# Half of a weight block moved behind a run of shuffle transfers on the load queue

## The chip, the core and the metric

The kernel runs on one core of a Trainium2 chip. Its engines work side by side: TensorE (PE; PEld is its weight load), VectorE (DVE), ScalarE (ACT), GpSimd (POOL) and SyncE (SP). Each has its own instruction list, and semaphores order them against each other. Transfers are issued by SyncE or by GpSimd and carried out by 16 DMA engines. The metric is the device time of one execution in microseconds; of several executions the median is given.

## The reference

The input x has 2048 positions of 448 channels, and so have k and v, all bf16. First comes a mixer: x + A(layernorm(x), k, v), with

```
k_shift[t] = sum over 4 taps of k[t - tap] * shift_k[tap]
kv         = k_shift * v
y          = causal convolution of kv with ssm_k along the 2048 positions, by a 4096-point FFT
A          = q * (y + kv * ssm_D)
h          = x + A(layernorm(x), k, v)
```

Then comes an MLP over positions rather than over channels:

```
u  = gelu(w1^T layernorm(h) + b1)     w1: 2048 x 1792
h2 = h + w2^T u + b2                  w2: 1792 x 2048
```

w1 and w2 are 7.34 MB each, in bf16. They are the bulk of what is read from memory.

## The kernel before, in words

The 2048 positions are laid out as 128 partitions by 16 rows. Everything lies in one large on-chip array, `arena`, so nearly all tiles are called `arena` in the profile; PSUM tiles are called `ps`.

The convolution is a two-stage Fourier transform by matrix products. A first stage works within each row (L933 for k, L885 and its neighbours for v), and its result is spread anew over the partitions by small transfers from on-chip memory to on-chip memory, the shuffles (L947). A second stage follows (L964). Then the spectra are multiplied on VectorE (L1015) and the first inverse stage runs on TensorE (L1027). ScalarE or VectorE copies its result out of PSUM (L652), and a second set of shuffles carries it to the buffer TZ. These are the inverse shuffles (L1037): 16 blocks, each with one transfer of 196 KB on GpSimd's queue and one of 28 KB on SyncE's. Every block writes a few partitions of all rows of TZ, so the second inverse stage (L1104) can begin on row 0 only when all blocks have arrived. To keep TensorE running meanwhile, 34 matmuls without a consumer (L1047) stand ahead of L1104.

After each row of the inverse transform, ScalarE and VectorE apply the gate and the residual (L1111, L1118), and with GpSimd's help the second layernorm (ending at L1159, which writes Q). The MLP's first product runs over 14 blocks of 128 output features. The first seven, from the left half of w1 (buffer W1A, 16 rows of 896 columns), are accumulated together: for each row, seven matmuls (L1203) that read that row of W1A and of Q. They are mixed with L1104 as rows of Q are completed. The other seven blocks, from the right half (W1B), follow one at a time, each over all 16 rows (L1213). Gelu is on ScalarE (L1193). The second product, 16 x 14 matmuls from W2, follows (L1223), then bias and residual (L1227) and the output transfers (L1231, L1234).

All weights are loaded by SyncE: W1A in four pieces of four rows (L1178), W1B in four (L1181), W2 in four (L1188). W1A is loaded before the inverse shuffles, W2 and W1B behind them.

The order of instructions on each engine comes from a planner that runs when the kernel is built. Each operation carries a due time, `sch.t0`. An engine takes, of the operations whose predecessors are done in the planner's model, the one with the highest priority:

```
prio[o.id] = prio[o.id] * 1e-6 - o.t0
```

so the earlier due time goes first, and the length of the path behind an operation only breaks ties. The argument `after` adds predecessors by hand. In `emit_w1_load` these come from `shuf`, which holds the shuffles by name: `shuf["upool15"]` is the last of GpSimd's shuffles of v's transform, and `shuf["zpool"]` the last of its inverse shuffles. The constants that matter here:

```
T_Q, T_DQ, T_I2, T_DI2, T_M1, T_W1 = 83.98, 14.35, 85.76, 0.401, 102.98, 122.45
T_CP, T_XL, T_WB = 20.0, -35.53, 154.44
```

W2's loads are due at T_W1 + 4.0 = 126.45 and wait for `shuf["zpool"]`. The numbers are only sort keys; they are not microseconds of the run.

Of the kernel before, what the change touches and what calls it, by code (L numbers as in the profile page):

```python
# [509 lines left out]
def _build(nc, A_q, A_k, A_v, A_shift_k, A_ssm_k, A_ssm_D, B_w1, B_b1, B_w2, B_b2, out):  # L510
# [27 lines left out]
    o_W1A = 0  # L538
# [27 lines left out]
    with ctx:  # L566
        sch = _Sched(nc, ctx, n_dma_sems=112, small_off=SMALL)
# [73 lines left out]
        T_Q, T_DQ, T_I2, T_DI2, T_M1, T_W1 = 83.98, 14.35, 85.76, 0.401, 102.98, 122.45  # L641

        T_TH, T_TN = -36.0, -30.0
        T_CP, T_XL, T_WB = 20.0, -35.53, 154.44
# [309 lines left out]
        shuf = {}  # L954
# [217 lines left out]

        def emit_w1_load(which):
            for h in range(4):
                sch.t0 = (T_W1, T_WB)[which] + 0.1 * h * (1 - which)
                rs = slice(4 * h, 4 * h + 4)
                if which == 0:
                    op(WQ, lambda e, W, rs=rs: e.dma_start(W1A[:, rs, :], w1d[:, rs, 0:896]),  # L1178
                       w=[(o_W1A + 4 * h * 1792, 4 * 1792)], dmab=128 * 4 * 1792, after=[shuf["upool15"]])
                else:  # L1180
                    op(WQ, lambda e, W, rs=rs: e.dma_start(W1B[:, rs, :], w1d[:, rs, 896:1792]),  # L1181
                       w=[(o_W1B + 4 * h * 1792, 4 * 1792)], dmab=128 * 4 * 1792, after=[shuf["zpool"]])
# [14 lines left out]
        def emit_mlp():  # L1197
# [21 lines left out]
            for r in range(R):  # L1219
# [19 lines left out]
                ("u1", emit_stage1, (V, o_V, TU, o_TU, "u")),    # L1239
                ("xload", emit_xload, ()), ("ct", emit_ct, ()), ("bias", emit_bias, ()), ("q", emit_q, ()),  # L1240
                ("u2", emit_stage2, (TU, o_TU, None)), ("i1", emit_products_i1, ()), ("w1a", emit_w1_load, (0,)), ("w1b", emit_w1_load, (1,)),
                ("warm", emit_warm, (N_WZ, T_I2 - 50.0, lambda: i1_last[-1:])),
                ("i2", emit_i2, ()), ("w2", emit_w2_load, ()), ("mlp", emit_mlp, ()))
# [39 lines left out]
```

## Time and profile before

| what | value |
|---|---|
| median of five runs | 191.09 us (189.79 to 191.66) |
| the profiled execution's own time | 191.09 us |
| its span, first to last instruction | 189.2 us |
| PE busy | 177.9 us (94%) |
| DVE busy | 110.0 us (58%) |
| ACT busy | 97.3 us (51%) |
| POOL busy | 72.1 us (38%) |
| mean granted TensorE clock | 0.973 |
| bytes moved by DMA | 35.43 MB, mean 187 GB/s |
| weight loads of W1 (L1178 and L1181) | 8 of 896 KB, median 13.1 us from issue to landing |
| weight loads of W2 (L1188) | 2 of 2048 KB, 10.4 us; 2 of 1536 KB, 17.5 us |

Times in the trace run from the first instruction. Busy time of PE is that of matmuls, which overlap, so 94% doesn't mean that 94% of its peak is reached. The page also shows the span in 40 slices of 4.73 us each, with the DMA engines' traffic in GB/s per slice. An engine's idle time before an instruction is put down to what ended it; that is the view that tells what waits for what.

### The profile page before, as it was taken

The numbers are of one execution on the slowest core, as the hardware profiler recorded it, in microseconds if no ns is written. First come the engines' busy times: TensorE is split into PE (matmuls) and PEld (weight loads), VectorE is DVE, ScalarE is ACT, GpSimd is POOL, SyncE is SP. The second block draws the span as 40 slices with busy tenths as digits, with TensorE's granted clock in tenths as the row PEclk, the third lists the DMA queues.
The fourth block names the chain that finished last, engine by engine and source line by source line (L and its number), as shares of the span: only waits on it lengthen the run. The fifth ranks groups of instructions, "written<-read, shape, count | busy, mean of one in ns | idle before, by whom it ended". The sixth has DMA issues, their size and how long they took to land.

```text
span 189.2 us, 2824 instructions
## 1 busy us (share of the span) xinstructions
PE 177.9 (94%) x1033; PEld 93.8 (50%) x1033; DVE 110.0 (58%) x181; ACT 97.3 (51%) x141; POOL 72.1 (38%) x176
## 2 busy tenths in 40 slices
PE   7999999899888998899989999999999999999993
PEld 2754443333332343234425444555556777777771
DVE  8867679898788999999788756100000222212221
ACT  3493979998799989970888384352121000000000
POOL 8933967799550015579169757000000000000000
PEclk9995599999999999999999999999999999999999
DMA  5996487778638998775799999000000100111111
GB/s 159 416 419 248 126 246 218 216 205 244 200 110 295 378 386 288 211 226 165 242 418 418 422 403 403 34 0 0 0 0 3 49 19 29 49 52 49 49 49 49
DMA packets 15724, 35.43 MB, mean 187 GB/s; under 512 B 3869, under 2 KB 9886, under 8 KB 15710
## 3 DMA queue, kind: packets, MB, share of 16 engines
q1 hardware_dynamic: 11102, 25.59, 35.9%
q0 software_dynamic: 4608, 9.66, 17.8%
q8 instruction: 8, 0.13, 0.3%
q14 instruction: 6, 0.05, 0.1%
HBM read 22.37 MB, written 1.84 MB: 128 GB/s over the span
## 4 chain that ended last, share of the span: by engine, by line
PE 82%; ACT 8%; DVE 6%; issue 2%
PE ps L1223 22%; PE ps L1213 11%; PE ps L1203 10%; PE ps L933 7%; PE ps L885 6%; PE ps L1047 5%; PE ps L1027 5%; ACT arena L652 4%; PE ps L964 3%; PE ps L1104 3%; PE ps L914 3%; PE ps L904 3%; ACT arena L943 2%; DVE arena L1015 2%; PE ps L996 1%
## 5 line engine op out<-in xcount | busy, mean ns | idle before, releaser
L1227 DVE SCALAR_TENSOR_TENSOR arena<-ps,arena 128x448 bf16<-128x448 f32 x16 | 10.9, 684 | 56.9 <-PE ps L1223 56.9
L1223 PE MATMUL ps<-arena 128*128 128x448 bf16 x224 | 42.5, 353 | 0.0
L1223 PEld LDWEIGHTS ps<-arena 128*128 128x128 bf16 x224 | 32.3, 144 | 10.1
L943 ACT CAST arena<-ps 128x896 bf16<-128x896 f32 x32 | 26.8, 930 | 5.7 <-PE ps L937 2.9
L652 ACT CAST arena<-ps 128x896 bf16<-128x896 f32 (+1 forms) x26 | 22.0, 909 | 2.9 <-PE ps L868 1.9
L1203 PE MATMUL ps<-arena 128*128 128x448 bf16 x112 | 23.0, 353 | 0.3 <-DVE arena L1159 0.2
L947 POOL DMA_DIRECT2D arena<-arena x32 | 19.2, 601 | 9.2 <-ACT arena L943 6.0
L1213 PE MATMUL ps<-arena 128*128 128x448 bf16 x112 | 21.4, 352 | 0.0
L933 PE MATMUL ps<-arena 128*128 128x448 bf16 x64 | 18.9, 416 | 0.4 <-ACT arena L943 0.2
L1193 ACT ACTIVATE arena<-ps,arena 128x448 bf16<-128x448 f32 x14 | 8.2, 639 | 20.1 <-PE ps L1213 14.7
L879 DVE TENSOR_TENSOR arena<-arena 128x1792 bf16<-128x1792 bf16 x16 | 18.3, 1178 | 0.0
L964 PE MATMUL ps<-arena 128*64 128x448 bf16 x128 | 16.4, 362 | 1.8 <-ACT arena L652 1.0
L1111 ACT ACTIVATE arena<-ps,arena 128x448 f32<-128x448 f32 x16 | 11.2, 722 | 12.0 <-PE ps L1104 9.0
L1037 POOL DMA_DIRECT2D arena<-arena x16 | 9.4, 594 | 20.8 <-PE ps L964 15.6
L1015 DVE TENSOR_TENSOR arena<-arena 128x1792 bf16<-128x1792 bf16 x16 | 16.4, 1083 | 0.0
L1203 PEld LDWEIGHTS ps<-arena 128*128 128x128 bf16 x112 | 10.9, 98 | 11.1 <-DVE arena L1159 1.3
L1213 PEld LDWEIGHTS ps<-arena 128*128 128x128 bf16 x112 | 10.9, 98 | 10.2
L885 PE MATMUL ps<-arena 128*128 128x448 bf16 x64 | 14.5, 354 | 1.5 <-ACT arena L943 0.9
L1027 PE MATMUL ps<-arena 64*128 64x448 bf16 x128 | 14.1, 352 | 1.3 <-DVE arena L1015 0.6
L1118 DVE SCALAR_TENSOR_TENSOR arena<-arena 128x448 f32<-128x448 bf16 x16 | 10.7, 677 | 4.5 <-ACT arena L1111 4.5
L933 PEld LDWEIGHTS ps<-arena 128*128 128x128 f16 x64 | 6.3, 109 | 10.0 <-issue 4.2
L964 PEld LDWEIGHTS ps<-arena 128*64 128x64 f16 x128 | 5.4, 108 | 11.4 <-ACT arena L652 4.6
(87 smaller groups left out, 206.0 us busy)
## 6 DMA issues: line engine op xcount, KB each, us to landing
arena<-arena POOLq DMA_DIRECT2D x48, 196.0 KB, 4.8
arena<-in_B_w_dram SPq DMA_DIRECT2D x8, 896.0 KB, 13.1
arena<-in_B_w_dram SPq DMA_DIRECT2D x2, 2048.0 KB, 10.4
arena<-in_B_w_dram SPq DMA_DIRECT2D x2, 1536.0 KB, 17.5
arena<-in_A_k_dram SPq DMA_DIRECT2D x4, 448.0 KB, 7.3
arena<-in_A_v_dram SPq DMA_DIRECT2D x4, 448.0 KB, 7.9
arena<-in_A_q_dram SPq DMA_DIRECT2D x4, 448.0 KB, 4.9
out_dram<-arena SPq DMA_DIRECT2D x7, 224.0 KB, 1.9
```

The lines of the kernel that those rows point to most:

```text
L652: return e.copy(out=dst(), in_=src())
L879: op("dve", lambda e, W, T=T, i=i, r=r: e.tensor_tensor(out=T[:, i], in0=KH[:, r:r + 4, :], in1=WT, op=ALU.mult), r=[(o_KH + r * DB, 4 * D ...
L885: op("pe", lambda e, W, b=b, T=T, i=i, j=j: e.matmul(Pb(b, i), ID, T[:, i, j, :], start=(j == 0), stop=(j == 3)), r=[(o_ID, 256), (o + (i ...
L933: op("pe", lambda e, W, b=b, r=r, h=h, dl=dl: e.matmul(Pb(b, h), E[:, 2 * r + h, :], src[:, r, :], start=True, stop=not dl), r=[r_E(r), (o ...
L943: return e.copy(out=dst, in_=Ppair(b)) if W == "act" else e.tensor_copy(out=dst, in_=Ppair(b))
L947: shuf[tag + q_ + str(r)] = shuf[tag + q_] = op(q_, lambda e, W, w=w, p0=p0, a=a, b_=b_, j0=j0: e.dma_start(T[p0:p0 + 29:4, j0:j0 + (b_ - ...
L964: op("pe", lambda e, W, b=bs[h], h=h, j=j, c=c, par=par: e.matmul(PS[64 * par:64 * par + 64, b.slots[c], 0:D], FW[:, 64 * c:64 * c + 64], ...
L1015: op("dve", lambda e, W, m=m, i=i: e.tensor_tensor(out=MR(m.slots[0]).rearrange("p (x y) d -> p x y d", x=2), in0=TU[:, i].unsqueeze(2).br ...
L1027: k = op("pe", lambda e, W, b=bs[h], m=ms[h], par=par, t=t, tab=tab, xy=xy, P=P: e.matmul(Pb(b, par), tab[P, :], MR(m.slots[0])[P, xy, :], ...
L1203: op("pe", lambda e, W, r=r, fc=fc, b=bs[fc]: e.matmul(Pb(b), W1A[:, r, 128 * fc:128 * fc + 128], Q[:, r, :], start=(r == 0), stop=(r == R ...
L1213: op("pe", lambda e, W, r=r, fc=fc, b=b: e.matmul(Pb(b), W1B[:, r, 128 * (fc - n0):128 * (fc - n0) + 128], Q[:, r, :], start=(r == 0), sto ...
L1223: op("pe", lambda e, W, r=r, fc=fc, b=b: e.matmul(Pb(b), W2[fc // 7][:, fc % 7, r:S:R], G[:, fc, :], start=(fc == 0), stop=(fc == NFC - 1) ...
```

## The change

The four loads of W1A no longer have one place. The first two (rows 0 to 7) keep theirs. The last two (rows 8 to 15) get a due time that is 30 lower, and wait for the last of GpSimd's inverse shuffles rather than for the last shuffle of v. The four loads of W1B get a due time that is 30 lower as well, 124.44, which is under that of W2 (126.45).

```diff
         def emit_w1_load(which):
             for h in range(4):
-                sch.t0 = (T_W1, T_WB)[which] + 0.1 * h * (1 - which)
+                sch.t0 = (T_W1 - 30.0 * (h > 1), T_WB - 30.0)[which] + 0.1 * h * (1 - which)
                 rs = slice(4 * h, 4 * h + 4)
                 if which == 0:
                     op(WQ, lambda e, W, rs=rs: e.dma_start(W1A[:, rs, :], w1d[:, rs, 0:896]),
-                       w=[(o_W1A + 4 * h * 1792, 4 * 1792)], dmab=128 * 4 * 1792, after=[shuf["upool15"]])
+                       w=[(o_W1A + 4 * h * 1792, 4 * 1792)], dmab=128 * 4 * 1792,
+                       after=[shuf["upool15" if h < 2 else "zpool"]])
```

As built, SyncE's list changes like this (lines as in the kernel before; after the change those behind the edit are one higher):

```
before: x load | 4 W1A | 16 shuffles | 4 W2 | 4 W1B | outputs
after:  x load | 2 W1A | 16 shuffles | 2 W1A | 4 W1B | 4 W2 | outputs
```

The lists of the other four engines keep their order and their waits. Only the semaphores by which TensorE waits for a load have other numbers.

## The prediction

> **What bounds the kernel now.** I began with the page's slices, to see who is busy where, and with the chain that ended last. The chain is TensorE for 82% of the span. Its pieces from 83 us on (start, length, what):
>
> ```profile
> 83.49 6.61 PE ps L1047 x34
> 90.09 1.53 PE ps L1104 x8
> ...
> 109.32 1.32 PE ps L1203 x7
> ...
> 114.37 8.12 PE ps L1203 x42
> 122.48 21.19 PE ps L1213 x112
> 143.67 42.39 PE ps L1223 x224
> 186.06 0.03 issue
> 186.08 0.68 DVE arena L1227
> ```
>
> From 114.37 us on, 42 + 112 + 224 = 378 matmuls take 71.7 us, 0.190 us each, with nothing between them. That stretch is pure TensorE time. A load can lengthen it by being late and cannot shorten it by being early. Ahead of it stands the hand-over from the inverse shuffles (L1037) to the inverse transform (L1104); between the two, TensorE runs 34 filler matmuls (L1047) that have no consumer.
>
> Next I asked who waits for a transfer between 60 and 130 us (engine, line, what it waited for; total us, times, longest):
>
> ```profile
> PEld ps L1104 <- ACT arena L1111: 3.3, 8, 0.9
> ...
> PEld ps L1203 <- DVE arena L1159: 1.3, 3, 0.7
> ...
> PEld ps L1104 <- DMA arena<-arena: 0.2, 1, 0.2
> ```
>
> The last line is the only compute wait on any transfer in these 70 us: 0.2 us, for the last shuffle. No engine waits for a weight.
>
> Then the load queue itself, in order of time (SyncE issues; start, length):
>
> ```profile
> 59.30 3.57 SPq L1178 DMA_DIRECT2D arena<-in_B_w_dram  x2
> 68.65 17.13 SPq L1037 DMA_DIRECT2D arena<-arena  x16
> 89.85 2.97 SPq L1188 DMA_DIRECT2D arena<-in_B_w_dram  x4
> 92.87 17.55 SPq L1181 DMA_DIRECT2D arena<-in_B_w_dram  x4
> ```
>
> (The first two W1A issues start at 58.1 us by the line's own record; the fourth starts at 60.19 and takes 2.68.) Last, traffic in four stretches (window; length, then PE, PEld, DVE, ACT, POOL; clock, DMA share, GB/s):
>
> ```profile
> 72.00:74.00 2.00, 1.92 (x20) 0.82 (x22) 2.00 (x3) 2.00 (x4) 0.79 (x2) 1.00 0.98 311
> 74.00:76.00 2.00, 2.00 (x24) 0.72 (x20) 1.97 (x2) 2.00 (x4) 1.17 (x2) 1.00 0.69 200
> ...
> 116.00:118.00 2.00, 2.00 (x13) 1.00 (x11) 0.84 (x2) 0.04 (x1) 1.64 (x5) 1.00 1.05 404
> 118.00:120.00 2.00, 2.00 (x12) 1.05 (x11) 0.93 (x2) 0.00 (x0) 0.00 (x0) 1.00 0.31 118
> ```
>
> The W1A load ends at about 74 us (issue at 60.2 plus its longest landing, 13.9, gives 74.1); after that the shuffles run alone at some 200 to 240 GB/s. The weight traffic behind the shuffles is full at 116 to 118 and gone soon after 118.
>
> **The change, part by part.** The diff does two things. Two of the four W1A issues (rows 8 to 15) move on SyncE from ahead of its 16 shuffles to behind them, with a wait for the last GpSimd shuffle. And because the due times T_WB - 30 and T_W1 - 30 both come out below W2's, the four W1B issues now stand ahead of W2's four. The instruction orders of PE, DVE, ACT and POOL are the same, waits on engines included; only the numbers of DMA semaphores change. So all that can differ is when transfers land.
>
> *Removed ahead of the shuffles.* Two transfers of 128 x 4 x 1792 B = 0.917 MB, 1.835 MB in all. Traffic ran at 366 to 400 GB/s from 60 to 70 us, so with 385 the first block's traffic ends 4.8 us earlier, near 69 us instead of 74. On SyncE the issue time of two DMAs goes (0.47 to 2.68 us each), but SyncE then idles 5.8 us for the first shuffle's data anyway (60.19 + 2.68 = 62.87 to 68.65): worth nothing. What do the shuffles get from emptier engines? Their time from issue to landing (min/median/max), for the four GpSimd shuffles issued beside the W1A traffic (68 to 74 us), and for the four issued at 80 to 84 us, without it:
>
> ```profile
> DMA to landing us min/median/max: 3.9/4.3/4.7
> ```
> ```profile
> DMA to landing us min/median/max: 3.8/4.2/4.6
> ```
>
> The difference is 0.1 us. [...] I take the row. [...] SyncE's own small shuffles (28 KB) stand behind W1A in the same queue and have no landing of their own in the trace; the earliest may be some us late now. Their readers come no earlier than 90 us, and the buffer that they free is not written before W2's second half: nothing again. The most that a faster last shuffle could give is the 0.2 us wait, because the fillers hold TensorE until 90.09. Gain: 0 to 0.2 us; I take 0.1.
>
> *The moved loads.* SyncE gets past the last shuffle's wait at 89.85 us, as now. Behind it stand the two W1A, four W1B and four W2 issues, then the outputs, whose first waits for DVE until 149.7. Today 11.01 MB follow the shuffles (4 x 0.917 + 2 x 2.097 + 2 x 1.573); they flow from about 92.1 to 118.6, which is 415 GB/s. The first W2 load landed 7.9 us after issue: 5.05 for its 2.097 MB at that rate, 2.3 to the start of the flow, 0.5 to finish. For pieces of the W1 kind I use the 385 of above:
> - W1A third quarter: 92.1 + 2.4 + 0.5 = 95.0 us; fourth: 97.4.
> - W1B, four pieces of 2.4: 99.8 to 107.0.
> - W2, 7.34 MB at 415 = 17.7: the last at 124.7.
>
> Who waits for these? L1203 takes rows in order, seven matmuls each. Counting PE's order, row 8's first is the sixth in the group of seven that starts at 109.16 in the timeline (109.32 in the chain, which counts from the end of the piece before), so 109.16 + 5 x 0.19 = 110.1 us; row 12's is the 15th of the 42 that start at 114.37, 117.1 us. Margins: 110.1 - 95.0 = 15 us and 117.1 - 97.4 = 20 us. W1B is first read at 122.5 and wholly by 125.5; it lands by 107.0, against roughly 120 now (the last issue at 108.3 plus the shortest landing, 12.1), so its margin grows by some 13 us. W2 is first read at 143.7 and wholly by 146.2: margin 19 us or more for the last piece. If it is the cover that I have wrong, each us beyond a margin costs a us, since TensorE has nothing else queued. [...]
>
> *Traffic beside other work.* The weights now flow six us longer, to about 125 us, beside the end of L1203 and the start of L1213. L1203 ran under 400 GB/s at 353 ns and its weight loads at 98; L1213, under none, at 352 and 98. VectorE's products (L1015) took 1.03 us each under W1A (three in 3.08) and 1.02 without (five in 5.09). Price: 0 for both, at most 3 x 0.01 us of gain.
>
> *The unknown.* No trace shows loads of two kinds queued as the new order queues them. The longest issue-to-landing of any weight piece is 20.7 us (a W1B piece behind 7.34 MB of W2). Were the third quarter as slow, it would land at 110.55 and cost 0.45 us. Bounds: 0 to 0.45 us slower on this side, and 0.2 us faster on the other; I take the near row, the first W2 load, and so 0.
>
> *Sum.* The profiled execution took 191.09 us: span 189.2 and 1.9 outside. It equals the median of the five runs. 191.09 - 0.1 + 0 = **191.0 us**.
>
> **Rivals.** *Faster: the shuffles are starved by W1A.* For it: DMA share is 1.0 and more from 60 to 72 us, just where the first shuffles start. Against it: landings of 4.3 and 4.2 us, and the 0.2 us wait. The ceiling is all idle time of TensorE from 58 to 84 us, 26.0 - 23.3 = 2.7 us: 188.4 us. It would need VectorE and ScalarE, on which those waits end, to speed up when traffic falls, and they don't.
>
> *Slower: row 8 comes late.* If the DMA engines served all ten loads together rather than in the order of issue, the third quarter would end with the last of them, at 124.7 instead of 95.0, and TensorE would stand from 110.1 to 124.7: 191.0 + 14.6 = 205.6 us. It decides from a landing after 110.1 us, and shows as over 1% from 112. Against it: the four W2 loads, issued within 2.7 us of each other, landed 7.9 to 18.9 us after issue, so one after another. A milder form, partly mixed service with a landing between 112 and 115, would give 193 to 196.
>
> *It doesn't do what it says.* Both parts are in SyncE's order, so this is out, except that the W1B and W2 exchange could matter more than the W1A move; with margins of 15 and 19 us it moves nothing either.
>
> **How the numbers follow.** No change: 0.88, at 191.0 us. Faster by over 1%: 0.05. Slower by over 1%: 0.07, the late row or something that the trace of before hasn't shown. One per cent, 1.9 us, is about the spread of this kernel's five runs (189.79 to 191.66) and so what a measurement can tell from nothing. The range is that spread around the sum: 189.8 less the 0.2 gain gives 189.6, and 191.7 plus the 0.45 cost gives 192.1.
>
> **What would show it.** In the changed profile: SyncE's first block with two L1178 issues near 58 us and two more at 89.9; slices 14 and 15 (66 to 76 us) down from 386 and 288 GB/s to roughly 270 and 220; slice 25 (118 to 123 us) up from 34 to about 400; GpSimd shuffle landings still near 4.2 to 4.9 us; L1047's fillers still ending at 90; no wait of L1204 or L1214 on a transfer; the last 378 matmuls still in 71.7 us. Wrong would be a wait on a DMA at row 8 of L1204 (a landing after 110), at L1224's first group (after 143.7), or filler matmuls that end before 89 because the products ran faster.

## The result, and the profile after

The changed kernel takes 190.49 us (median of 43 runs, 188.51 to 193.48), the kernel before 190.21 us (median of 80 runs, 187.59 to 193.31). The comparison gives a ratio of 1.004 with an interval of 1.0018 to 1.0061: 0.4% longer, where 0.1 us shorter was forecast. The time lies in the forecast range and within the 1% that was called no change, but the interval excludes the forecast sign, and that has to be explained.

One thing has to be known to read that number: the comparison leaves out, for each kernel, the runs more than 1.5% above that kernel's own fastest, and since 80 runs found a faster fastest (187.59) than 43 did (188.51), the cut falls at 190.40 us for one kernel and at 191.34 us for the other. The means of what is left are 189.17 and 189.92 us, whose ratio is the 1.0040. With one cut for both kernels the same runs give 1.0008 (both cut at 190.40 us) or 1.0005 (both at 191.34). The means of all runs are 190.21 and 190.34: 1.0007, with an interval of 0.998 to 1.003 when the runs are drawn anew. So most of the 0.4% is made by the two cuts, and the experiments had to tell whether anything is left.

The end of the chain in the changed kernel (start, length, what), to set beside that of before:

```profile
84.73 4.56 DMA arena<-arena
...
89.33 1.70 PE ps L1104 x8
...
113.78 8.12 PE ps L1204 x42
121.90 21.19 PE ps L1214 x112
143.09 42.39 PE ps L1224 x224
185.47 0.02 issue
185.50 0.68 DVE arena L1228
```

The start of the inverse transform on TensorE, before and after (start, length; idle time of over 0.15 us ahead of a piece would stand in brackets at its end):

```profile
83.49 6.61 PE L1047 MATMUL ps<-arena 128*128 128x448 f16 x34
89.93 1.68 PE L1104 MATMUL ps<-arena 128*128 128x448 bf16 x8
```
```profile
82.64 6.61 PE L1047 MATMUL ps<-arena 128*128 128x448 f16 x34
89.33 1.69 PE L1104 MATMUL ps<-arena 128*128 128x448 bf16 x8
...
108.57 1.49 PE L1204 MATMUL ps<-arena 128*128 128x448 bf16 x7
```

From the first inverse matmul (L1104) to the last addition it is 185.50 - 89.33 = 96.17 us; before it was 186.08 - 89.93 = 96.15. That is the whole stretch in which the moved loads run and are read, and it hasn't changed. One link is new: the chain now passes through the last shuffle (4.56 us) rather than through the filler matmuls (L1047). The two end at nearly the same moment, and here the shuffle ended last. From the first filler to the first inverse matmul it is now 89.33 - 82.64 = 6.69 us, where it was 89.93 - 83.49 = 6.44. The waits of 60 to 130 us show the same:

```profile
PEld ps L1104 <- ACT arena L1111: 3.4, 8, 0.9
...
PEld ps L1204 <- DVE arena L1159: 1.3, 3, 0.7
...
PEld ps L1104 <- DMA arena<-arena: 0.5, 1, 0.5
```

Still no engine waits for a weight. The weight load (PEld) of the first inverse matmul waits 0.5 us for the last shuffle, where it was 0.2. SyncE's queue (start, length):

```profile
57.27 1.02 SPq L1178 DMA_DIRECT2D arena<-in_B_w_dram  x2
67.81 17.13 SPq L1037 DMA_DIRECT2D arena<-arena  x16
89.31 0.93 SPq L1178 DMA_DIRECT2D arena<-in_B_w_dram  x2
90.27 5.17 SPq L1182 DMA_DIRECT2D arena<-in_B_w_dram  x4
95.48 11.45 SPq L1189 DMA_DIRECT2D arena<-in_B_w_dram  x4
```

By the landing records of these loads, the third and fourth quarters of W1A arrive at 94.27 and 96.83 us, W1B from 99.01 to 106.47, and the last of W2 at 123.86. SyncE got past the shuffles at 89.31, 0.54 us earlier than in the sum. With that taken off, the forecast 95.0, 97.4, 99.8 to 107.0 and 124.7 were met within 0.3 us.

The traffic per slice of 4.7 us:

```profile
GB/s 154 420 416 257 127 207 255 238 219 240 185 106 343 395 51 187 206 219 157 269 396 401 422 420 419 400 9 0 0 0 3 49 27 22 49 52 49 49 49 49
```

Slice 14 (66 to 71 us) fell from 386 to 51, slice 15 from 288 to 187, and slice 25 (118 to 123 us) rose from 34 to 400. I had expected about 270 and 220 for the first two. The second quarter of W1A landed at 68.34 us after an issue at 57.76, and the first shuffles begin only at 69.6, so the engines are nearly empty in between.

### The profile page after: what moved, and what is told of

Read it like the earlier page. It is cut to its first block, busy times and chain, and to the rows that moved or that the text cites. A ratio compares the mean times of both kernels' runs of the same rounds, so it can differ in the third digit from the quotient of the medians.

```text
span 188.6 us, 2824 instructions
## 1 busy us (share of the span) xinstructions
PE 176.1 (93%) x1033; PEld 92.8 (49%) x1033; DVE 110.0 (58%) x181; ACT 97.0 (51%) x141; POOL 70.9 (38%) x176
## 4 chain that ended last, share of the span: by engine, by line
PE 72%; ACT 8%; DMA 6%; DVE 5%; POOL 4%; issue 2%; ACTq 0%; POOLq 0%
PE ps L1224 22%; PE ps L1214 11%; PE ps L1204 10%; DMA arena<-arena 6%; PE ps L1027 5%; ACT arena L652 4%; PE ps L964 4%; PE ps L914 3%; PE ps L1104 3%; PE ps L904 3%; PE ps L885 3%; PE ps L933 3%; POOL arena L947 2%; ACT arena L943 2%; PE ps L1047 2%
## 5 line engine op out<-in xcount | busy, mean ns | idle before, releaser
L1224 PE MATMUL ps<-arena 128*128 128x448 bf16 x224 | 42.5, 353 | 0.0
L1204 PE MATMUL ps<-arena 128*128 128x448 bf16 x112 | 23.0, 353 | 0.3 <-DVE arena L1159 0.2
L1214 PE MATMUL ps<-arena 128*128 128x448 bf16 x112 | 21.4, 353 | 0.0
L933 PE MATMUL ps<-arena 128*128 128x448 bf16 x64 | 16.0, 355 | 1.3 <-ACT arena L943 1.3
L1204 PEld LDWEIGHTS ps<-arena 128*128 128x128 bf16 x112 | 10.8, 98 | 11.1 <-DVE arena L1159 1.3
L885 PE MATMUL ps<-arena 128*128 128x448 bf16 x64 | 14.5, 354 | 1.8 <-ACT arena L943 1.2
L1214 PEld LDWEIGHTS ps<-arena 128*128 128x128 bf16 x112 | 10.9, 98 | 10.2
L655 DVE CAST arena<-ps 128x896 bf16<-128x896 f32 (+2 forms) x11 | 9.5, 876 | 2.7 <-PE ps L868 1.2
```

The lines of the kernel that those rows point to most:

```text
L885: op("pe", lambda e, W, b=b, T=T, i=i, j=j: e.matmul(Pb(b, i), ID, T[:, i, j, :], start=(j == 0), stop=(j == 3)), r=[(o_ID, 256), (o + (i ...
L933: op("pe", lambda e, W, b=b, r=r, h=h, dl=dl: e.matmul(Pb(b, h), E[:, 2 * r + h, :], src[:, r, :], start=True, stop=not dl), r=[r_E(r), (o ...
L1204: op("pe", lambda e, W, r=r, fc=fc, b=bs[fc]: e.matmul(Pb(b), W1A[:, r, 128 * fc:128 * fc + 128], Q[:, r, :], start=(r == 0), stop=(r == R ...
L1214: op("pe", lambda e, W, r=r, fc=fc, b=b: e.matmul(Pb(b), W1B[:, r, 128 * (fc - n0):128 * (fc - n0) + 128], Q[:, r, :], start=(r == 0), sto ...
L1224: op("pe", lambda e, W, r=r, fc=fc, b=b: e.matmul(Pb(b), W2[fc // 7][:, fc % 7, r:S:R], G[:, fc, :], start=(fc == 0), stop=(fc == NFC - 1) ...
```

## The experiments

The last GpSimd shuffle is the hinge. For each kernel below two stretches are given from the timeline: from the start of the first filler to the first inverse matmul ("hand-over"), and from there to the start of the last addition ("tail"). The "landing" is the time of that shuffle from issue to arrival. A ratio is that to the kernel before, measured beside it; the theories are numbered in the expectations.

### Each half of the change alone, and the move doubled

The move alone (W2 stays ahead of W1B); edit of the kernel before:

```diff
-                sch.t0 = (T_W1, T_WB)[which] + 0.1 * h * (1 - which)
+                sch.t0 = (T_W1 - 30.0 * (h > 1), T_WB)[which] + 0.1 * h * (1 - which)
...
-                       w=[(o_W1A + 4 * h * 1792, 4 * 1792)], dmab=128 * 4 * 1792, after=[shuf["upool15"]])
+                       w=[(o_W1A + 4 * h * 1792, 4 * 1792)], dmab=128 * 4 * 1792,
+                       after=[shuf["upool15" if h < 2 else "zpool"]])
```

> Only the second half of W1A moves behind the shuffles; W2 stays ahead of W1B. Theory 1 (no part of the change reaches the time; up to 0.3 us by a later last shuffle): ratio 0.998 to 1.002, and TensorE's first inverse matmul starts 6.4 to 6.7 us after the first filler. Theory 2 (the shuffles end later when less W1A traffic runs ahead of them): the whole cost is here, ratio about 1.004, +0.8 us. Theory 3 (the exchange of W1B and W2 costs): ratio 1.000. Last W1A quarter lands near 97 us, last W1B piece near 124.

Measured: 190.13 us, ratio 1.0035 (1.0001 to 1.0069). The hand-over took 7.18 us, outside what theory 1 allowed and near the 0.8 us that theory 2 asked for; the next kernels tell more of that. And the tail grew by 0.3 us, for a reason that no theory of mine had named. The end of the chain and one wait:

```profile
113.37 12.11 DMA arena<-in_B_w_dram
125.53 19.09 PE ps L1214 x100
144.62 42.39 PE ps L1224 x224
```
```profile
PEld ps L1214 <- DMA arena<-in_B_w_dram: 0.6, 1, 0.6
```

With W2 still ahead of it and 1.83 MB more in front, the last piece of W1B lands at 125.48 us, a little after the 13th matmul of L1214 would have read it. So the exchange of W1B and W2 is what makes room for the move: by the records of the kernel before, W1B's last piece arrived at 120.38 us and was first read by the 13th matmul of L1213, at 122.32 + 12 x 0.19 = 124.6. Those 4.2 us are less than the 4.4 that 1.83 MB take at 415 GB/s.

The exchange alone; edit of the kernel before:

```diff
-                sch.t0 = (T_W1, T_WB)[which] + 0.1 * h * (1 - which)
+                sch.t0 = (T_W1, T_WB - 30.0)[which] + 0.1 * h * (1 - which)
```

> All of W1A stays ahead of the shuffles; only W1B goes ahead of W2. Theory 1: ratio 0.998 to 1.002. Theory 2: ratio 1.000, first inverse matmul 6.4 us after the first filler as in the kernel before. Theory 3: ratio about 1.004, with a wait on a transfer or slower matmuls in the MLP.

Measured: 189.15 us, ratio 0.9973 (0.9935 to 1.001). Hand-over 6.50, tail 96.17. No cost of the exchange shows.

All four quarters behind the shuffles; edit of the changed kernel:

```diff
-                sch.t0 = (T_W1 - 30.0 * (h > 1), T_WB - 30.0)[which] + 0.1 * h * (1 - which)
+                sch.t0 = (T_W1 - 30.0, T_WB - 30.0)[which] + 0.1 * h * (1 - which)
...
-                       after=[shuf["upool15" if h < 2 else "zpool"]])
+                       after=[shuf["zpool"]])
```

> All four quarters of W1A stand behind the shuffles, so no weight traffic runs beside them: the move doubled. The quarters should land at 95.0, 97.4, 99.8 and 102.2 us; rows 0, 4, 8, 12 are first read at 95.7, 101.9, 110.1 and 117.1, so at most the first is near a wait. Theory 1: ratio 0.998 to 1.003 (a first row late by up to 0.5 us). Theory 2: twice the cost, ratio about 1.008, and the first inverse matmul more than 6.9 us after the first filler. Theory 3: ratio 1.004.

Measured: 189.59 us, ratio 1.001 (0.9974 to 1.0045). Hand-over 6.49, tail 96.16. Twice the move shows no cost, although the first quarter now lands at 93.68 and is first read at 94.75. Theory 2 asked for 1.008 and a hand-over above 6.9 us; it falls.

### The measurement against itself

No edit: the kernel before, under another name.

> The kernel before, instruction for instruction, measured as if it were a changed one. Theory 4 (the 0.4% is how the runs of a kernel that scatters by 1.2 us are picked and averaged, not the change): the ratio may leave 1 by 0.2 to 0.4% either way although nothing differs. Theories 2 and 3: 1.000 with an interval that holds 1, and e1 or e2 stands apart from it. In this trace as in the others the time from the first filler matmul to the end should be 105.7 us within 0.3, and the scatter lie ahead of it.

Measured: 190.41 us, ratio 0.9957 (0.9922 to 0.9992). Hand-over 6.44, tail 96.15. The same instructions differ from themselves by as much as the changed kernel did, with an interval that excludes 1, and over all runs their ratio is 0.9994. So an interval of this kind doesn't carry 0.4% for a kernel whose runs spread from 188 to 193 us.

And the changed kernel a second time, again with no edit:

> The changed kernel as it is, looked at and timed a second time. Theory 1: first inverse matmul 6.44 to 6.5 us after the first filler in this look. Theory 5: 6.7 or more again. Theory 4: the ratio of its runs moves from 1.004 by up to 0.4% although nothing has changed; by all of its runs it should lie within 0.2% of 1.

Measured: 190.19 us, ratio 0.9994 (0.996 to 1.0029); 1.004 did not come back. The two measurements of the changed kernel together hold 65 runs with a mean of 190.33 us, beside 131 runs of the kernel before with a mean of 190.33: ratio 1.000, 0.998 to 1.002 when drawn anew. But the hand-over was late again in this profile (from TensorE's timeline; the last field is what it waited for):

```profile
81.06 6.61 PE L1047 MATMUL ps<-arena 128*128 128x448 f16 x34
88.17 1.69 PE L1104 MATMUL ps<-arena 128*128 128x448 bf16 x8 [0.50 <-DMA arena<-arena]
```

88.17 - 81.06 = 7.11 us where the kernel before had 6.44. That was worth following.

### Does W1A's place set the landing of the last shuffle?

Two kernels with 20 fillers in place of 34, so that the landing shows bare; the edit is the same in both:

```diff
-        N_WZ, N_WI, N_W0, N_WK, N_WJ = 34, 6, 9, 3, 8
+        N_WZ, N_WI, N_W0, N_WK, N_WJ = 20, 6, 9, 3, 8
```

> The kernel before with 20 filler matmuls (L1047) ahead of the inverse transform rather than 34, so that they end about 3.9 us after their start and the landing of the last shuffle shows bare. Theory 1: TensorE then waits some 2.4 us for it and starts the first inverse matmul 6.2 to 6.5 us after the first filler; time as before within 0.5 us. Theory 2 needs the same here, and more in the changed kernel's twin.

> The changed kernel with 20 fillers. Theory 1 (landing does not depend on W1A's place): first inverse matmul 6.2 to 6.5 us after the first filler, as in its twin, and the same time within 0.3 us. Theory 5 (with just half of W1A ahead, the last shuffle lands 0.2 to 0.7 us later, as in the profiles of the changed kernel and of the move alone): 6.7 to 7.2 us after the first filler, and 0.3 to 0.7 us longer than the twin.

Measured: 191.99 us, ratio 1.0036 (0.9978 to 1.0095), for the kernel before with 20 fillers; 191.63, ratio 1.002 (0.9981 to 1.0059), for the changed one. Hand-overs 7.02 and 7.23. The first speaks against theory 5: all of W1A is ahead, and the shuffle lands late too, after 4.89 us (5.09 in the changed kernel). Both kernels also lost 2 us in the tail, 98.16 against 96.16, which I had not expected; it comes last in this document.

Other amounts ahead: first one quarter of W1A (edit of the changed kernel):

```diff
-                sch.t0 = (T_W1 - 30.0 * (h > 1), T_WB - 30.0)[which] + 0.1 * h * (1 - which)
+                sch.t0 = (T_W1 - 30.0 * (h > 0), T_WB - 30.0)[which] + 0.1 * h * (1 - which)
...
-                       after=[shuf["upool15" if h < 2 else "zpool"]])
+                       after=[shuf["upool15" if h < 1 else "zpool"]])
```

> One quarter of W1A ahead of the shuffles, three behind. So far the last GpSimd shuffle landed 4.2, 4.3, 4.4 and 4.9 us after its issue with all four quarters ahead, 4.6, 5.0, 5.0, 5.0 and 5.1 with two, 4.35 with none. Theory 5 (the less W1A traffic ahead of or beside the shuffles, the later the last one lands): 4.9 us or more here, first inverse matmul 7.0 us or more after the first filler. Theory 6 (the landing scatters by some 0.3 us from one execution to the next for reasons outside the change): anything between 4.2 and 5.1. Time within 0.3% of before under both.

Then three quarters, the same edit with `h > 2` and `h < 3`:

> Three quarters of W1A ahead, one behind. Theory 5: landing between that of four and of two, about 4.7 us. Theory 6: anything between 4.2 and 5.1. Time within 0.3% of before under both.

And all of W1A behind, with 20 fillers:

> All of W1A behind the shuffles and 20 fillers: the third of a set with the two kernels of 20 fillers, whose last shuffle landed after 4.9 us (all ahead) and 5.1 us (half ahead). Theory 5: 5.1 us or more. Theory 6: anything between 4.2 and 5.1. Time as in those two, 191.5 to 192 us.

Measured: 189.05 us, ratio 0.9959 (0.9925 to 0.9993), with one quarter ahead; 190.24, 0.9991 (0.9956 to 1.0026), with three; 191.1, 1.0072 (1.0037 to 1.0106), with none and 20 fillers. Landings of the last shuffle: 4.77, 4.63 and 4.79 us. No order by the amount ahead. (The first interval excludes 1 on the faster side; after the kernel against itself I read nothing from that.)

Then both kernels in turn on one chip, unchanged:

> The kernel before, one more look. Theory 5 (W1A's place sets the landing): the last GpSimd shuffle lands 4.2 to 4.5 us after its issue, first inverse matmul 6.4 to 6.5 us after the first filler. Theory 6 (scatter): 4.2 to 5.1 us, as in the changed kernel's looks.

> The changed kernel, one more look. Theory 5: the last shuffle lands 4.9 to 5.1 us after its issue, first inverse matmul 6.9 to 7.2 us after the first filler. Theory 6: 4.2 to 5.1 us.

> As for the first look at the kernel before: 4.2 to 4.5 us by theory 5, 4.2 to 5.1 us by theory 6.

> As for the first further look at the changed kernel: 4.9 to 5.1 us by theory 5, 4.2 to 5.1 us by theory 6.

Measured in this order, one execution each: 188.89, 188.20, 188.82 and 189.29 us. Landings 4.54, 4.27, 4.65 and 4.40 us: the changed kernel's were the earlier ones. Theory 5, which asked for 4.9 us or more with half of W1A ahead, falls in that form. Here are the kernels with all 34 fillers and W1A split 4-0 or 2-2 (quarters ahead and behind). Sets 1, 2 and 4 ran on one chip each; set 3, on a fourth, held the kernels with one, three and no quarters ahead:

| set | kernel | W1A | landing | hand-over | tail |
|---|---|---|---|---|---|
| first profiles | before | 4-0 | 4.26 | 6.44 | 96.15 |
| | after | 2-2 | 4.56 | 6.69 | 96.17 |
| 1 | before itself | 4-0 | 4.22 | 6.44 | 96.15 |
| | exchange alone | 4-0 | 4.37 | 6.50 | 96.17 |
| | move alone | 2-2 | 5.03 | 7.18 | 96.46 |
| 2 | after, second time | 2-2 | 4.96 | 7.11 | 96.16 |
| 4 | before, two profiles | 4-0 | 4.54, 4.65 | 6.68, 6.78 | 96.16, 96.17 |
| | after, two profiles | 2-2 | 4.27, 4.40 | 6.44, 6.53 | 96.16, 96.17 |

The hand-over is the landing plus 2.14 us, but never under 6.44: that is where the inverse transform starts when only the fillers hold it. (The fillers' record is 6.61 us long; the profile models the ends of matmuls, and the next one starts inside it.) In set 2 all four kernels landed between 4.89 and 5.09 us, one with all of W1A ahead and three with half; in set 4 all lay between 4.27 and 4.65. There the landing goes with the set, but not in set 1, where 5.03 us stands beside 4.22, 4.37 and, with all four quarters behind, 4.35. Over all sets, with the kernels of 20 fillers and the one with the half last (5.04 us, below), the mean landing is 4.49 us for 4-0 (six profiles) and 4.76 for 2-2 (seven), each with a scatter of about 0.3. So a delay of some 0.3 us from the move is neither shown nor excluded, and what makes a landing late stays open.

### What sharing costs a shuffle

In the prediction, shuffles beside W1A were read as landing as fast as others. To test that, W1B was put ahead of the shuffles too, so that weight traffic runs beside nearly all of them. (The planner was told smaller sizes for these loads, so that all other engines keep their order. Edit of the kernel before.)

```diff
-                sch.t0 = (T_W1, T_WB)[which] + 0.1 * h * (1 - which)
+                sch.t0 = (T_W1, T_W1 + 1.0)[which] + 0.1 * h * (1 - which)
...
-                       w=[(o_W1B + 4 * h * 1792, 4 * 1792)], dmab=128 * 4 * 1792, after=[shuf["zpool"]])
+                       w=[(o_W1B + 4 * h * 1792, 4 * 1792)], dmab=4 * 1792, after=[shuf["upool15"]])
```

> W1B goes ahead of the shuffles as well (eight transfers, 7.34 MB), so that weight traffic runs beside nearly all shuffles and not only beside the first four. If sharing costs a shuffle nothing, as the row of the four early ones was read in the prediction, the last one lands after 4.2 to 5.1 us and the time stays within 0.3%. [...]

Measured: 194.47 us, ratio 1.0217 (1.0159 to 1.0275). The landings of the shuffles issued from 80 to 84 us, and the hand-over:

```profile
DMA to landing us min/median/max: 7.2/7.4/7.4
```
```profile
82.76 6.61 PE L1047 MATMUL ps<-arena 128*128 128x448 f16 x34
92.31 3.17 PE L1104 MATMUL ps<-arena 128*128 128x448 bf16 x8 [2.95 <-DMA arena<-arena]
```

7.4 us where the kernel before had 4.2, and a hand-over of 9.55 us. The first GpSimd shuffle, with none of its kind ahead of it, took 5.9 us where it took 3.1 in the changed kernel. So sharing had a price here, about 3 us for a shuffle (7.4 - 4.2 and 5.9 - 3.1). How the engines divide their time between the two queues, no run here shows. In the prediction unlike was set beside like: the four early shuffles, issued from 70.46 to 72.20 us, met only the last 2 to 4 us of W1A (landed at 74.06), and the later ones had other shuffles ahead of them. The proper partners are the same four without W1A. In the changed kernel's profile, those issued from 67 to 73 us:

```profile
DMA to landing us min/median/max: 3.1/4.3/4.9
```

Here only the first clearly gained, from 3.9 to 3.1 us. Another pair of profiles shows a larger price for the same four: with 20 fillers they took 5.2 to 5.6 us beside all of W1A, and 3.1 to 4.9 with half of it ahead. The two numbers in the prediction could show neither.

### What a late quarter costs

The second half of W1A behind all other weights, TensorE's order kept (again by smaller sizes told to the planner; edit of the changed kernel):

```diff
-                sch.t0 = (T_W1 - 30.0 * (h > 1), T_WB - 30.0)[which] + 0.1 * h * (1 - which)
+                sch.t0 = (T_W1 + 30.0 * (h > 1), T_WB - 30.0)[which] + 0.1 * h * (1 - which)
```

> The second half of W1A goes behind all other weights, TensorE's order kept. If the loads are served in the order of issue, as the prediction took it, the third quarter lands near 122 us rather than 95, row 8 is late by 122 - 110 = 12 us, and the time is about 202 us: each us beyond the margin costs a us. If the loads are served together, it lands only a few us later than in the changed kernel, and the time stays under 195 us.

Measured: 203.23 us, ratio 1.072 (1.0645 to 1.0795). TensorE at row 8:

```profile
107.77 1.11 PE L1204 MATMUL ps<-arena 128*128 128x448 bf16 x5
121.07 0.91 PE L1204 MATMUL ps<-arena 128*128 128x448 bf16 x2 [12.19 <-DMA arena<-in_B_w_dram]
```

The third quarter landed at 120.93 us, and the wait was 12.19 us, as expected for loads that land in the order of issue. In the profiles of before and after all twelve do (from 66.07 to 120.38 us and from 64.98 to 123.86), so here the order on SyncE's queue decides. The tail grew by 13.77 us, 1.6 more than the wait; the last section has a likely reason.

## Why the prediction was right or wrong

**The tail: right.** The last 378 matmuls take 71.7 us in both profiles, and the tail is 96.15 and 96.17 us. Nothing of the moved traffic is felt there.

**The landings of the weights: right,** within 0.3 us. The danger of a late row 8 is real, as the kernel with the half last shows, but far: the third quarter lands at 94.27 us, and row 8 is first read at 108.57 + 5 x 0.19 = 109.5, so the margin is the forecast 15 us. I judged the exchange to be without effect because the margins on both sides were 15 and 19 us. Those were the margins after the change. Without the exchange, W1B's margin of 4.2 us would have gone, as the move alone showed. The exchange protects the move.

**The price of sharing: wrong.** "The difference is 0.1 us ... I take the row" is the faulty step; the price was some 3 us where a shuffle shared all its time, with W1B ahead too. It did no harm to the sum because the last shuffle was issued at 85.58 us in the profile of before, 11.5 us after W1A had landed (74.06).

**The step that failed: "Gain: 0 to 0.2 us; I take 0.1".** This term alone gave the forecast a sign, and it is worth nothing. The 0.2 us were a wait of the weight load beside fillers that still ran. In the timeline of before, the first inverse matmul starts at 89.93 us with no idle time ahead of it, so an earlier shuffle could not have started it sooner. The table says the same: landings of 4.22, 4.26 and 4.27 us all give a hand-over of 6.44. Nor did less traffic ahead bring the shuffle in earlier: with none at all it landed after 4.35 us.

The term was also bounded on one side only. The cover by the fillers is flush: a landing later than about 4.3 us passes to the end undiminished, in either kernel. The kernel before happened to be profiled at 4.26 us, and that single profile was taken as its value, while with all 34 fillers and no weights beside it the landing scatters from 4.22 to 5.04 us here. At the hand-over that is up to 0.74 us later (7.18 against 6.44). By the table the mean hand-over is 6.59 us for the kernel before (6.44, 6.44, 6.68, 6.78) and 6.69 for the changed one (6.69, 7.11, 6.44, 6.53): 0.1 us apart, with a scatter of 0.2 to 0.3 in each.

**The measured 0.4%.** Most of it comes from the two cuts: with one cut for both it is 0.05 to 0.08%. It did not return in the second measurement, and the kernel before against itself gave 0.4% to the other side. Over all 65 and 131 runs the ratio is 1.000 (0.998 to 1.002). The executions with a mean granted TensorE clock of 0.995 or more, where it is on record, have a mean of 189.88 us for the changed kernel (46 of 65) and of 189.69 for the kernel before (128 of 191): 1.0010, and 0.9991 to 1.0028 when drawn anew. So the runs allow anything from 0.2% faster to 0.3% slower, or about 0.5 us, and a delay of 0.1 to 0.3 us at the hand-over would be hidden in that. The scatter of the profiles lies mostly ahead of the change: the first filler starts anywhere from 80.59 to 83.51 us, while the tail holds to 0.02 us wherever all fillers stand and no weight or last shuffle is late by microseconds. So the forecast of no change stands, and the forecast of a sign did not deserve to be made.

**The base.** The sum started from 191.09 us, 0.9 us above the median of the 80 runs of the same kernel. It was an execution with the clock halved for 10.24 us far ahead of the change, as the last section shows. That the measured time still lies in the range is owed to the range's width of 2.5 us.

## What to carry to other kernels

When two things release the same instruction at nearly the same time, cost a change to either on both sides: the cover here, with no slack, passed on the delays (landings of 4.37 to 5.03 us, hand-overs of 6.50 to 7.18) and no gain (landings of 4.22 to 4.27 us, all 6.44). A wait of the weight load is not yet a wait of the matmul (0.2 us and none in the profile of before); read the matmul's own idle time. Compare a shared transfer with the same transfer alone, not with another one that waits in its own queue. And before a difference of a few tenths of a per cent is explained, measure the unchanged kernel against itself and cut both kernels' runs at the same time; where the scatter lies ahead of the change, the length of the stretch behind it in the trace is the sharper measure.

## What the runs showed of the hardware

Here a gap in TensorE cost more than itself. With 20 fillers TensorE stood for 3 us before the first inverse matmul; in the kernel before with that edit the timeline reads

```profile
83.11 3.96 PE L1047 MATMUL ps<-arena 128*128 128x448 f16 x20
90.13 2.44 PE L1104 MATMUL ps<-arena 128*128 128x448 bf16 x8 [3.07 <-DMA arena<-arena]
92.64 2.12 PE L1047 MATMUL ps<-arena 128*128 128x448 f16 x6
```

and the windows behind it (length, PE, PEld, DVE, ACT, POOL; granted clock, DMA share, GB/s)

```profile
91.00:93.00 2.00, 1.94 (x7) 0.47 (x6) 1.52 (x4) 2.00 (x4) 0.00 (x0) 0.50 0.90 231
93.00:94.00 1.00, 1.00 (x4) 0.43 (x3) 1.00 (x4) 0.34 (x1) 0.00 (x0) 0.50 1.01 389
...
95.00:96.00 1.00, 0.94 (x6) 0.32 (x5) 0.92 (x5) 0.82 (x2) 0.49 (x2) 1.00 0.98 397
```

The granted clock drops to 0.50. By the trace's clock records it does so for 3.41 us, from 90.91 to 94.32, and it does so in all four kernels with a gap of 2.95 to 3.27 us here: the three with 20 fillers and the one with W1B ahead. The drop begins 2.4 to 4.3 us after the end of the last filler. In none of the others, with gaps of 0.6 us or less, does it drop here. The tail grows by 1.5 to 2.0 us (97.66 to 98.16 against 96.16). At 0.50 there are 7 matmuls in 2.00 us, at 1.00 there are 6 in 1.00 us. So, as an estimate, half a clock over the 2.8 to 3.4 us of it in which TensorE runs is worth at most 1.4 to 1.7 us, and explains most of the growth; the rest is open. The medians of the three kernels with 20 fillers lie 1.0 to 1.4 us above that of the kernel before in their set, although TensorE waits for the same shuffle. In the kernel with the half last the clock was halved as well, for 10.24 us from 113.83 on, which reaches 3 us past the end of its wait (five matmuls of L1204 took 1.88 us there, and 1.11 ahead of the wait); that fits its extra 1.6 us. What fixes the start and the length of a drop is not shown. Where W1B stays behind the shuffles, 34 fillers hide the last one but for 0.6 us or less, and no drop shows at the hand-over.

The clock also tells a part of the scatter. The granted clock in 40 slices, before and after:

```profile
PEclk9995599999999999999999999999999999999999
```
```profile
PEclk9999999999999999999999999999999999999999
```

In the profile of before it is halved for 10.24 us from 13.29 us on; the matmuls of L933, which run there, took 416 ns in the mean, and 355 after. Four of the 18 profiles have such a drop at 13.3 to 13.7 us, of 6.83 or 10.24 us, in kernels of both orders. A drop of 10.24 us makes a mean clock of 1 - 5.12 / 189.2 = 0.973, the value of that execution. Executions with a mean under 0.995 took 191.37 us (63 of the 191 of the kernel before that have it on record) and 191.44 us (19 of the 65 of the changed one), some 1.6 us more than the others. What sets the drop off in some executions is not shown, and the others still scatter from 187.6 to 192.4 us.
